# Converting two row blocks of a weight at a time, with a reordered start and extra products of ones

## The chip, the cores and the metric

The kernel runs on one core of a Trainium2 chip. The metric is the device time of one execution in microseconds (us). TensorE (PE) does matrix products and transposes, VectorE (DVE), ScalarE (ACT) and GpSimd (POOL) work on tiles of 128 partitions in SBUF, and SyncE (SP) issues the DMAs here. Each engine runs its own instructions in a fixed order and waits on semaphores for the others.

## The reference

Three layers follow each other on 4 batches of 576 positions with 512 channels:

```
scores = where(causal, -1e9, q k^T / 8 + min(-(cum_i - cum_j), 0))     # 32 heads of 64
attn   = softmax(scores) v                                             # cum = cumsum(relu(s))
xk, xr = mu * x + (1 - mu) * shift(x)                                  # token mix, x = attn
x2     = sigmoid(xr w_r) * (relu(xk w_k)^2 w_v)
u, v   = split(gelu(x2 w_in));  v_n = layernorm(v) * g_ln
out    = x2 + (u * (w_sg v_n + b_sg)) w_out
```

q, k, v and s are float32. The weights w_k, w_r, w_v, w_in and w_out arrive as float64, seen by the kernel as pairs of 32-bit words.

## The kernel before

Attention runs over 16 pairs of heads. The scores of a pair go through two PSUM tiles, VectorE adds the mask, scales and takes the minimum in one instruction (`fold`, L363; a second short instruction reads its accumulator), ScalarE takes the exponential (L389), PE transposes the rows and multiplies them by v. The first batch is done in two rounds of four pairs: pairs 0 to 3 with query blocks 0 to 2, then the same pairs with blocks 3 and 4. I number the folds from the start of the program; fold 20 ends the first round, fold 44 the second, and folds 45 to 50 open the second batch.

The next layer (`moe1`, L663 for its products) works in eight units of 288 columns. A product is made exact by splitting both sides into a high and a low float32r part and adding three products. Its operations are drawn in between those of attention, by a generator; a rate sets how many attention steps are taken per product, and a dependency without a semaphore puts the products of `moe1` behind the attention product issued last. The order in each queue is then settled by a scheduler with priorities.

Each weight has to be converted from float64 words to high and low parts (`convert`). For a 128-row block of 512 columns this takes seven instructions: ScalarE takes the absolute value of the high words (L111), VectorE bounds it (L115), shifts and masks (L116), puts in sign and exponent (L117) and the low word's bits (L118), ScalarE copies the high part, VectorE subtracts it (both through helpers, L71 and L74). The temporary `cvt` lives in the place of the tile `rt`, which `moe1` needs later. The 20 blocks of w_k, w_r and w_v are converted while the first batch's attention runs, w_in (8) and w_out (4) later. A VectorE copy of one element (L101) ties the load of a later block to a point in VectorE's order.

At the start, GpSimd clears the mask and the identity and selects their triangles, VectorE makes the running sum of s, and 18 products of ones (L246) occupy PE.

## Time and profile before

| quantity | value |
|---|---|
| runs | 703.83, 707.19 and 918.62 us, median 707.19 us |
| profiled execution | 701.49 us, of which the span of its instructions is 699.7 us |
| PE busy in the span | 663.8 us (95%) |
| DVE busy | 510.3 us (73%) |
| ACT busy | 406.5 us (58%) |
| POOL busy | 234.2 us (33%) |
| mean granted TensorE clock | 0.975 of full speed |

The shares are averages over stages. For a stage, read its own stretch: which engine is busy all the time there, and what the others wait for. A wait of an engine that has nothing urgent to do costs nothing.

### The profile page before, as it was taken

To read this page: it belongs to the slowest core of one execution; us is meant where nothing else is said; L and a number is where in the kernel's file an instruction comes from. 1 tells how busy PE (TensorE), PEld (TensorE's weight loads), DVE (VectorE), ACT (ScalarE), POOL (GpSimd) and SP (SyncE) were. 2 spreads that over 40 slices of the span, in tenths; PEclk is the share of its full clock that TensorE was granted. 3 is DMA by queue.
4 is the path that set the end of the run, shared out by engine and by line. 5 is a ranking of instruction groups with operands and counts; after the bars stand their busy time and mean duration, and the time that the engine had idled before them with its cause. 6 is when DMAs were issued, how large, how long until landed. Compare 5 with 4: busy or idle time off the path is not lost.

```text
span 699.7 us, 12939 instructions
## 1 busy us (share of the span) xinstructions
PE 663.8 (95%) x4598; PEld 624.9 (89%) x4598; DVE 510.3 (73%) x1227; ACT 406.5 (58%) x979; POOL 234.2 (33%) x232
## 2 busy tenths in 40 slices
PE   6888969999999989999899999999999999999998
PEld 3666969998998989999899989999998998998997
DVE  8989996887888887688776798744856564664543
ACT  5779767878878876888595544624523233233120
POOL 7024465645755765585542262120000000000000
PEclk8899968999999999999999999999999999999999
DMA  8996333344443333433201700004230300300101
GB/s 239 291 208 211 111 116 88 87 149 118 127 125 105 99 88 108 121 97 96 80 23 48 281 32 35 1 18 164 76 102 18 119 1 16 121 1 9 60 2 68
DMA packets 39833, 67.48 MB, mean 96 GB/s; under 512 B 6909, under 2 KB 23401, under 8 KB 39737
## 3 DMA queue, kind: packets, MB, share of 16 engines
q1 hardware_dynamic: 39768, 66.66, 32.1%
q8 instruction: 36, 0.59, 0.4%
q14 instruction: 29, 0.23, 0.1%
HBM read 51.85 MB, written 10.19 MB: 89 GB/s over the span
## 4 chain that ended last, share of the span: by engine, by line
PE 69%; ACT 7%; DVE 6%; DMA 2%; issue 1%; SPq 1%; POOL 0%; DVEq 0%; ACTq 0%; POOLq 0%
PE m L663 26%; PE po L676 7%; PE pu L676 7%; PE av L513 3%; PE t L528 3%; PE pg L914 2%; PE pg L915 2%; PE pg L913 2%; PE pv L851 2%; PE pv L852 2%; PE pv L850 2%; ACT pr L389 2%; PE s L348 2%; PE s L349 2%; DVE xf L602 1%
## 5 line engine op out<-in xcount | busy, mean ns | idle before, releaser
L74 POOL TENSOR_TENSOR xl<-xf,xh 128x288 fp32r<-128x288 f32 x64 | 70.1, 1106 | 88.8 <-ACT xh L71 47.7
L389 ACT ACTIVATE pr<-pr,nm 128x448 f32<-128x448 f32 (+4 forms) x144 | 84.9, 590 | 14.7 <-DVE nm L363 13.1
L663 PE MATMUL m<-xh,wk 128*128 128x288 f32 x512 | 81.6, 298 | 0.0
L663 PE MATMUL m<-kh,wv 128*128 128x288 f32 x512 | 80.1, 297 | 0.0
L363 DVE CUSTOM_DVE_ANT_0 pr<-s,mask 128x448 f32<-128x448 f32 (+4 forms) x144 | 63.6, 453 | 17.3 <-PE s L349 8.9
L663 PEld LDWEIGHTS m<-xh,wk 128*128 128x128 f32 x512 | 71.9, 189 | 0.9
L663 PEld LDWEIGHTS m<-kh,wv 128*128 128x128 f32 x512 | 71.8, 189 | 0.6
L348 PE MATMUL s<-qk 128*128 128x288 f32 (+4 forms) x144 | 46.8, 327 | 7.8 <-DVE nm L363 6.0
L602 DVE SCALAR_TENSOR_TENSOR xf<-xt,mu_sb,xf 128x288 f32<-128x288 f32 x64 | 47.3, 744 | 6.5 <-ACT xf L596 6.1
L532 DVE TENSOR_TENSOR ptl<-t,pth 128x512 fp32r<-128x512 f32 (+1 forms) x72 | 44.2, 616 | 7.0 <-ACT pth L531 6.8
L71 ACT CAST xh<-xf 128x288 fp32r<-128x288 f32 (+1 forms) x80 | 36.1, 480 | 22.4 <-DVE xf L602 13.7
L663 PE MATMUL m<-xl,wk 128*128 128x288 f32 x256 | 47.7, 299 | 0.0
L74 POOL TENSOR_TENSOR qk<-qld,qk 64x576 fp32r<-64x576 f32 (+1 forms) x28 | 39.2, 1401 | 21.2 <-DVE qk L71 9.4
L531 ACT CAST pth<-t 128x512 fp32r<-128x512 f32 (+1 forms) x72 | 37.9, 531 | 13.4 <-PE t L528 12.6
L349 PE MATMUL s<-qk 128*128 128x288 f32 (+4 forms) x144 | 44.6, 313 | 0.0
L596 ACT ACTIVATE xf<-xt,mu 128x288 f32<-128x288 f32 x64 | 33.9, 535 | 17.0 <-POOL xl L74 16.3
L663 PE MATMUL m<-kl,wv 128*128 128x288 f32 x256 | 43.4, 299 | 0.0
L624 ACT ACTIVATE kf<-m 128x288 f32<-128x288 f32 x64 | 26.0, 410 | 29.9 <-PE m L663 28.6
L663 PE MATMUL m<-xh,wr 128*128 128x288 f32 x256 | 40.5, 300 | 1.2 <-ACT rt L637 0.9
L676 PE MATMUL pu<-xh,wi 128*128 128x288 f32 x256 | 40.5, 296 | 0.2 <-ACT ut L876 0.2
L71 ACT CAST gh<-gf 128x288 fp32r<-128x288 f32 x32 | 13.9, 433 | 46.2 <-DVE gf L920 46.2
L528 PE MATMUL t<-ident,pr 128*128 128x128 f32 x252 | 39.1, 276 | 0.4 <-DVE ptl L532 0.2
(299 smaller groups left out, 1840.2 us busy)
## 6 DMA issues: line engine op xcount, KB each, us to landing
kld<-qkv SPq DMA_DIRECT2D x28, 288.0 KB
qld<-qkv SPq DMA_DIRECT2D x24, 288.0 KB
x_d<-rt SPq DMA_DIRECT2D x8, 576.0 KB
xf<-x_d SPq DMA_DIRECT2D x8, 576.0 KB
outT<-ot SPq DMA_DIRECT2D x32, 144.0 KB
vld<-qkv SPq DMA_DIRECT2D x24, 160.0 KB
qk<-qk SPq DMA_DIRECT2D x24, 144.0 KB
rb<-rd SPq DMA_DIRECT2D x24, 128.0 KB
```

The lines of the kernel that those rows point to most:

```text
L71: nc.scalar.copy(dst, src) if eng == "A" else nc.vector.tensor_copy(dst, src)
L74: (nc.gpsimd if pick(engines) == "P" else nc.vector).tensor_tensor(dst, a, b.bitcast(F32), ALU.subtract)
L348: nc.tensor.matmul(dst, qk[0][:, 0, qs], qk[0][:, 1, ks], start=True, stop=False)
L349: issued[0] = nc.tensor.matmul(dst, qk[1][:, 0, qs], qk[1][:, 1, ks], start=False, stop=True)
L363: nc.vector.tensor_tensor_reduce(out=dst, in0=src, in1=msk, scale=-0.125, scalar=first, op0=ALU.add, op1=ALU.min, accum_out=acc)
L389: i = nc.scalar.activation(dst, dst, AF.Exp, bias=nm[:, col : col + 1], scale=-1.0, accum_out=w.sm[:, col : col + 1])
L528: issued[0] = nc.tensor.transpose(bank[:, o : o + P], x, ident)
L531: nc.scalar.copy(pth[:, cols], bank[:, 0:o])
L532: nc.vector.tensor_tensor(ptl[:, cols], bank[:, 0:o], pth[:, cols].bitcast(F32), ALU.subtract)
L602: nc.vector.scalar_tensor_tensor(xf, xc, mu_sb[:, j, c : c + 1], xf, ALU.mult, ALU.add)
L663: i = nc.tensor.matmul(dst, w(x, c, m), xx[:, c], start=(n + c == 0), stop=(n == 2 and c == w.nk - 1))
L676: nc.tensor.matmul(dst, w(x, c, m), xx[:, c], start=(n + c == 0), stop=(n == 2 and c == w.nk - 1))
```

## The change

1. A weight's part now covers two row blocks. It is loaded by two DMAs into one tile and converted by seven instructions of 1024 elements instead of fourteen of 512. So w_k, w_r and w_v have 10 parts, w_in 4 and w_out 2. The look-ahead of loads goes from 5 blocks to 3 parts, and the rates at which conversions are drawn are halved (`C0`, `n % 2`, `n1`).
2. The temporaries move from the place of `rt` to tiles `xo0` and `xo1`, where the attention output of batches 1 and 3 will lie. Those tiles now hold two columns of 128 channels each; the even batches keep four tiles `xt0` to `xt3`, single-buffered.
3. The mask and the identity are cleared by VectorE instead of GpSimd, and the late clears of `qk` on GpSimd are put behind the two selections.
4. In the first four pairs, two products of ones follow each step's scores, 40 in all.
5. The first six absolute values are put behind an exponential each. The places for w_sg's parts change to suit the larger tiles.

```diff
-C0, RATE, LEAD, AHEAD = 0.7, 1.1, 0.0, 5
+C0, LEAD, AHEAD = 0.35, 0.0, 3
+GC = 6
+WJ, WN = 4, 2
-SLOTS = [("wk11", "wk21"), ("wk31", "wr00"), ("wr10", "wr20"), ("xh",), ("xl",)]
+SLOTS = ["wk01", "wk11", "wr00", "xh"]
...
-        raw = pool.tile([P, 512], I64, tag=name, name=name + "w")
+        raw = pool.tile([P, 2, 512], I64, tag=name, name=name + "w")
...
-            nc.vector.tensor_copy(raw.bitcast(F32)[:p, 0:1], after[:, 0:1])
-        nc.sync.dma_start(raw, src)
+            nc.vector.tensor_copy(raw.bitcast(F32)[:p, :, 0:1], after[:, 0:1].unsqueeze(1).to_broadcast([p, 2, 1]))
+        for i in range(2):
+            nc.sync.dma_start(raw[:, i], src[i * P : (i + 1) * P])
...
-        words = raw.bitcast(I32).rearrange("p (n t) -> p n t", t=2)
+        words = raw.bitcast(I32).rearrange("p c (n t) -> p (c n) t", t=2)
...
-        if GC and len(exps) > LC and done[0] < 2:
-            kind = mybir.DependencyInfo(mybir.DependencyClass.NoSync, mybir.DependencyReason.DATA)
-            tc.add_manual_dep(i.ins, exps[-1 - LC].ins.name, kind)
+        if 0 < len(exps) <= GC:
+            behind(i, exps[-1])
...
-        half = pool.tile([P, 2, 512], F32R, tag=name, name=name)
-        copy("A" if att is not None else "D", half[:, 0], t)
-        minus(ENG["cl"], half[:, 1], t, half[:, 0])
+        half = pool.tile([P, 2, 2, 512], F32R, tag=name, name=name)
+        hi, lo = (half[:, x].rearrange("p c n -> p (c n)") for x in range(2))
+        copy("A" if att is not None else "D", hi, t)
+        minus(ENG["cl"], lo, t, hi)
...
+        for i in i if eng is nc.gpsimd else ():
+            behind(i, made)
...
-    nc.gpsimd.memset(mask, 0.0)
+    nc.vector.memset(mask, 0.0)
...
-    make_identity(nc, ident)
+    nc.vector.memset(ident, 0.0)
+    made = nc.gpsimd.affine_select(
+        out=ident, in_=ident, compare_op=ALU.not_equal, fill=1.0, base=0, pattern=[[-1, P]], channel_multiplier=1
+    )
...
             exps.append(i)
+            if w.n < WJ:
+                for _ in range(WN):
+                    behind(nc.tensor.matmul(idle[:, 0:384], ones[:, 0:P], ones, start=True, stop=True), issued[0])
...
-                while w.p >= 8 and (w.p // 4 - 2, n % 4) not in mixed:
+                while b > 1 and not {(b - 2, x) for x in ((c, c + 1 - c % 2) if b % 2 else (c,))} <= mixed:
                     yield "wait"
-                w.xt = xtp.tile([P, S + 1], F32, tag=f"xt{n % 4}", name=f"xt{n % 4}", bufs=2)
-                xts.setdefault(w.p // 4, []).append(w.xt)
+                x = xts.setdefault(b, [])
+                if b % 2 == 0:
+                    x.append(xtp.tile([P, S + 1], F32, tag=f"xt{c}", name=f"xt{c}", bufs=1))
+                elif c % 2 == 0:
+                    two = xtp.tile([P, 2, S + 1], F32, tag=f"xo{c // 2}", name=f"xo{c // 2}", bufs=1)
+                    x += [two[:, 0], two[:, 1]]
...
-    temps = mw.tile([P, 2, 512], F32, tag="rt", name="cvt")
+    temps = [xtp.tile([P, 1024], F32, tag=f"xo{i}", name="cvt", bufs=1) for i in range(2)]
...
-            if n < 7:
+            if n < 7 and n % 2 == 0:
                 step(cvs, PC)
...
-    temps = w1p.tile([P, 2, 512], F32, tag="wk01", name="cvt")
-    cos = conversions([(wo, i, 0) for i in range(4)], lambda i: temps[:, i % 2])
+    temps = w1p.tile([P, 2, 1024], F32, tag="wr10", name="cvt")
+    cos = conversions([(wo, i, 0) for i in range(2)], lambda i: temps[:, i])
```

GpSimd at the start, before. `gt` is a table of bias rows, `qk_86` and `qk_87` are operand tiles, L255 is the mask's selection and masks.py:199 that of the identity:

```order
L254 MEMSET mask 128x768
masks.py:197 MEMSET ident 128x128
L159 MEMSET qk_87 64x640
...
L358 MEMSET sm 128x16
L718 MEMSET xt_262 128x1
L718 MEMSET xt_375 128x1
L255 ISA
L255 AFFINE_SELECT mask<-mask 128x128
masks.py:199 AFFINE_SELECT ident<-ident 128x128
```

GpSimd at the start, now (L264 and L275 are the selections):

```order
L166 MEMSET qk_87 64x640
L370 MEMSET sm 128x16
...
L478 MEMSET rcp 128x128
L307 MEMSET gt 48x576
L308 MEMSET gt 48x576
L307 MEMSET gt 48x576
L308 MEMSET gt 48x576
L167 MEMSET qk_87 1x640
L264 ISA
L264 AFFINE_SELECT mask<-mask 128x128
L275 AFFINE_SELECT ident<-ident 128x128
```

Two clears left GpSimd and eight went behind the selections, but four clears of `gt` and some small ones came ahead of them.

VectorE from fold 40 on, before. `pr_91`, `pr_90` and `pr_89` are the rows of scores that a fold writes, `cvt` the temporary, `wv_...` a converted block of w_v, `qk_1084` an operand of the next attention stage, `avt` and `sm` belong to attention:

```order
L118 SCALAR_TENSOR_TENSOR cvt<-wv50w,cvt 128x512
L398 RECIPROCAL rc<-sm 128x8
L115 TENSOR_SCALAR cvt<-cvt 128x512
L363 ISA pr_90,nm<-s,mask 128x448
...
L116 TENSOR_SCALAR cvt<-cvt 128x512
L74 TENSOR_TENSOR wv_823<-cvt,wv_823 128x512
L117 SCALAR_TENSOR_TENSOR cvt<-wv60w,cvt 128x512
L118 SCALAR_TENSOR_TENSOR cvt<-wv60w,cvt 128x512
L115 TENSOR_SCALAR cvt<-cvt 128x512
L455 TENSOR_TENSOR avt<-av,rc 128x256
L363 ISA pr_91,nm<-s,mask,nh 128x288
```

VectorE from fold 38 on, now:

```order
L118 SCALAR_TENSOR_TENSOR cvt<-wv30w,cvt 128x1024
L74 TENSOR_TENSOR qk_1027<-kld,qk_1026 64x576
...
L375 ISA pr_91,nm<-s,mask,nh 128x288
L375 ISA nm 128x1
L71 CAST qk_1026<-qld 128x576
L74 TENSOR_TENSOR wv_829<-cvt,wv_829 128x1024
L617 SCALAR_TENSOR_TENSOR xf<-xt_359,mu_sb,xf 128x288
L375 ISA pr_91,nh<-s,mask 128x288
```

The last conversion instruction now stands at fold 40, the last one before stood at fold 48; 11 of the 100 stood behind fold 40, now 1 of 50 (the L74 shown).

PE in the first pair, now. L358 is a product of scores, L439 a transpose, L407 the added products of ones:

```order
L358 MATMUL s<-qk_86 128x192
L407 LDWEIGHTS ones
L407 MATMUL warm<-ones 128x384
L407 LDWEIGHTS ones
L407 MATMUL warm<-ones 128x384
L439 MATMUL t<-ident,pr_89 128x128 x2
L439 MATMUL t<-ident,pr_88 128x128
```

Apart from these 40 pairs of rows the products of `moe1` and those of the scores stand in the same places to each other as before.

## Rows read from the trace of the kernel before

**Rows 1.** Windows by stage: busy time and instructions of each engine, granted clock, DMA.

```profile
20.00:60.00 40.00, 31.99 (x167) 23.30 (x167) 37.81 (x124) 32.59 (x90) 7.78 (x12) 0.92 0.99 267
69.00:90.00 21.00, 18.87 (x145) 18.36 (x145) 20.93 (x43) 16.27 (x38) 10.13 (x9) 1.00 0.43 129
113.00:700.00 587.00, 573.72 (x4096) 551.60 (x4096) 405.04 (x953) 322.45 (x770) 184.34 (x158) 1.00 0.26 79
```

**Rows 2.** Windows from the second round's end on, columns as in Rows 1.

```profile
89.70:98.86 9.16, 3.92 (x19) 2.88 (x19) 9.16 (x18) 6.30 (x13) 8.09 (x7) 0.75 0.34 96
98.86:111.33 12.47, 12.47 (x57) 12.27 (x57) 10.27 (x23) 7.64 (x17) 5.75 (x5) 0.50 0.30 83
111.33:117.50 6.17, 5.46 (x46) 5.15 (x45) 4.22 (x13) 4.75 (x13) 1.43 (x2) 1.00 0.29 86
```

**Rows 3.** Timeline of VectorE, first round: start, busy us, line, operation.

```profile
31.48 0.14 DVE L101 COPY wr20w<-cvt 128x1 f32<-128x1 f32 x1
31.55 0.68 DVE L118 SCALAR_TENSOR_TENSOR cvt<-wk11w,cvt 128x512 int32<-128x512 int32 x1
32.15 0.68 DVE L74 TENSOR_TENSOR wk<-cvt,wk 128x512 fp32r<-128x512 f32 x1
32.75 0.14 DVE L101 COPY wr30w<-cvt 128x1 f32<-128x1 f32 x1
...
33.95 0.42 DVE L115 TENSOR_SCALAR cvt<-cvt 128x512 f32<-128x512 f32 x1
34.29 0.48 DVE L363 CUSTOM_DVE_ANT_0 pr<-s,mask 128x320 f32<-128x320 f32 x1
```

**Rows 4.** Groups by shape, VectorE, 0 to 115 us: busy, mean ns, idle before.

```profile
L115 DVE TENSOR_SCALAR cvt<-cvt 128x512 f32<-128x512 f32 x20 | 12.3, 613 | 0.7 <-ACT cvt L111 0.7
L363 DVE CUSTOM_DVE_ANT_0 pr<-s,mask 128x448 f32<-128x448 f32 x9 | 5.4, 605 | 0.0
L363 DVE CUSTOM_DVE_ANT_0 pr<-s,mask 128x128 f32<-128x128 f32 x4 | 1.1, 279 | 0.0
```

**Rows 5.** Timeline of VectorE, two instructions of which the second needs the first.

```profile
55.65 0.84 DVE L117 SCALAR_TENSOR_TENSOR cvt<-wr20w,cvt 128x512 int32<-128x512 int32 x1
56.52 1.11 DVE L118 SCALAR_TENSOR_TENSOR cvt<-wr20w,cvt 128x512 int32<-128x512 int32 x1
```

**Rows 6.** Timeline of all engines, start of the kernel.

```profile
1.46 0.59 DVE L158 MEMSET qk<- 64x640 f32 x1 [0.19 <-issue]
1.93 0.20 POOL masks.py:197 MEMSET ident<- 128x128 f32 x1
2.13 0.59 DVE L159 MEMSET qk<- 64x640 f32 x1
5.39 0.74 POOL L255 TENSOR_SCALAR_AFFINE_SELECT mask<-mask 128x128 f32<-128x128 f32 x1
8.54 0.49 DVE L363 CUSTOM_DVE_ANT_0 pr<-s,mask 128x320 f32<-128x320 f32 x1
11.09 0.66 ACT L111 ACTIVATE cvt<-wk10w 128x512 f32<-128x512 f32 x1 [1.81 <-DMA wk10w<-w_k]
12.21 0.56 ACT L389 ACTIVATE pr<-pr,nm 128x320 f32<-128x320 f32 x1
```

**Rows 7.** Timeline of PE's weight loads beside the products of ones, start of the kernel.

```profile
5.14 0.15 PEld L246 LDWEIGHTS <-ones 128*128 128x128 bf16 x1 [0.17 <-issue]
5.46 0.63 PEld L246 LDWEIGHTS <-ones 128*128 128x128 bf16 x4 [0.17 <-issue]
```

**Rows 8.** Timeline of PE, groups of eight products at either speed.

```profile
87.89 1.22 PE L663 MATMUL m<-xh,wr 128*128 128x288 f32 x8
...
99.90 1.81 PE L432 MATMUL av<-vb,pth 128*128 128x64 f32 x8
113.75 1.00 PE L432 MATMUL av<-vb,pth 128*128 128x64 f32 x8
...
117.50 1.28 PE L663 MATMUL m<-xh,wr 128*128 128x288 f32 x8
```

**Rows 9.** Windows of 4 us, first round, columns as in Rows 1.

```profile
8.00:12.00 4.00, 1.63 (x6) 0.85 (x6) 3.21 (x15) 1.84 (x5) 3.71 (x11) 1.00 0.97 216
12.00:16.00 4.00, 2.02 (x8) 1.26 (x8) 3.96 (x14) 3.66 (x13) 1.93 (x4) 0.55 0.92 282
56.00:60.00 4.00, 2.73 (x15) 1.61 (x15) 3.97 (x12) 4.00 (x10) 1.20 (x2) 1.00 0.80 263
```

More of the change, by code (lines that the diff above doesn't have):

```diff
@@ L231, in block_kernel @@
     fetch(-1)
-    for c in range(max(1, E1)):
-        load_words(wk, c % 4, c // 4)
+    load_words(wk, 0, 0)
     gate_d = dram.tile([48, 2, 4, S], F32, name="gate_d")
@@ L288, in block_kernel @@
             rest(x, a, b, nc.gpsimd, nc.gpsimd)
-    for c in range(max(1, E1), AHEAD):
-        load_words(wk, c % 4, c // 4, after=cur)
+    for c in range(1, AHEAD):
+        load_words(wk, c % 2, c // 2, after=cur)
     tc.cur_priority += SECOND + GT
@@ L751, in block_kernel @@
     att = attend()
[L752 to L758 removed]
+    temps = [xtp.tile([P, 1024], F32, tag=f"xo{i}", name="cvt", bufs=1) for i in range(2)]
     cvs = conversions(
[L761 to L762 removed]
+        [(wk, c, n) for n in range(2) for c in range(2)] + [(wr, c, 0) for c in range(2)] + [(wv, c, 0) for c in range(4)],
+        lambda i: temps[i % 2],
         loaded=AHEAD,
@@ L833, in block_kernel @@
             temps = w2.tile([P, 5, 512], F32, tag="vt", name="cvt")
-            lws = conversions([(wi, c, n) for n in (1, 0) for c in range(4)], lambda i: temps[:, i % 5])
-            lws = chain(lws, x_load(0))
-        if w2 is not None and n % PACE == 0:
-            next(lws, None)
+            lws = conversions([(wi, c, n) for n in (1, 0) for c in range(2)], lambda i: temps[:, i % 2 * 2 : i % 2 * 2 + 2].rearrange("p c n -> p (c n)"))
+            lws, n1 = chain(lws, x_load(0)), 0
+        if w2 is not None:
+            n1 += 1
+            if n1 % PACE == 1 and n1 // PACE % 2 == 0 or n1 > 8 * PACE and n1 % PACE == 1:
+                next(lws, None)
     for _ in lws:
@@ L889, in norm @@
         nc.vector.tensor_tensor(rs, rs, t1, ALU.mult)
-        vh, vl = ([xtp.tile([P, DM], F32R, tag=f"xt{t}", name=n) for t in range(4)] for n in ("vh", "vl"))
+        vh = [xtp.tile([P, DM], F32R, tag=f"xt{t}", name="vh", bufs=1) for t in range(4)]
+        vl = [xtp.tile([P, 2, DM], F32R, tag=f"xo{t}", name="vl", bufs=1) for t in range(2)]
+        vl = [vl[t // 2][:, t % 2] for t in range(4)]
         v4 = const.tile([P, DM], F32R, tag="mask", name="v4")
@@ L937, in block_kernel @@
         nc.gpsimd.memset(mv[:, 4], 1.0)
+    places = [w1p.tile([P, 3, S], F32R, tag=t, name="wg") for t in SLOTS[:3]]
+    places = [x[:, i] for x in places for i in range(3)] + [xtp.tile([P, S], F32R, tag=SLOTS[3], name="wg")]
     wg = [[], []]
-    for c, tags in enumerate(SLOTS):
-        if len(tags) == 2:
-            halves = [w1p.tile([P, S], F32R, tag=t, name=f"wg{c}") for t in tags]
-        else:
-            place = xtp.tile([P, 2, S], F32R, tag=tags[0], name=f"wg{c}")
-            halves = [place[:, 0], place[:, 1]]
+    for c in range(5):
+        halves = places[2 * c : 2 * c + 2]
         for hf in range(2):
```

37 lines of the change are left out of this document (17 added, 20 removed).

## The prediction

> **What bounds the kernel now.** I read the windows by stage first, since the busy shares of the whole span mix stages with different limits. From 113 us on PE is busy 573.7 of 587.0 us at the granted clock 1.00 [rows 1]: that part is PE's, and time saved before it moves its end by as much, since its products stay the same. Before that VectorE is the full engine: 37.8 of 40 us from 20 to 60, and 20.9 of 21 from 69 to 90, with PE idle for 8.0 and 2.1 us [rows 1]. What fills it is the conversion of w_k, w_r and w_v beside the folds of attention. Then comes a stretch of another kind [rows 2]. From 89.7 to 98.9 us VectorE is full and PE has work for 3.9 of 9.2 us; by its end the clock has fallen. From 98.9 to 111.3 PE is busy all the time at the granted clock 0.50, which is 1.2 GHz, and VectorE has 2.2 us free. Eight products of 64 columns take 1.81 us there and 1.00 us at 113.75 [rows 8]. So the first 113 us are VectorE's, but for some 12 us that belong to PE at half speed.
>
> **The change, part by part.**
>
> *Merged conversions.* A VectorE step from one instruction's start to the next is 0.60 us for 512 elements (31.55, 32.15, 32.75) and 0.34 us for the bounding L115, which takes two elements at a time (33.95 to 34.29) [rows 3]. Folds of 448 and 128 elements take 605 and 279 ns [rows 4], so an element costs 326/320 = 1.02 ns, 512 cost 0.52 us, and 0.60 - 0.52 = 0.08 us of a step is fixed; for L115 it is 0.34 - 0.26 = 0.08 again. Of the three weights, 20 blocks with five VectorE instructions each become 10 parts: 100 instructions become 50, on a full engine. That removes 50 x 0.08 = 4.0 us. The copies that tie the loads go from 15 to 8, at steps of 0.07 us (31.48 to 31.55) [rows 3]: 0.5 us. ScalarE's 40 instructions become 20, but it is busy 32.6 of 40 us [rows 1], less than VectorE, so I count nothing.
>
> The VectorE page of the Trainium skill (VectorE: DVE Perf Modes, section The TRN2 errata) gives a fixed term of about 150 cycles per instruction, 156 ns at its 0.96 GHz. By that alone the merge would save 50 x 0.156 = 7.8 us. The folds' durations agree with the page (279 - 128 x 1.02 = 148 ns), the steps don't, because the next instruction starts 0.08 us before the end of the last [rows 3]; the sum goes by the steps.
>
> *Clears on VectorE.* Clearing 640 columns takes a step of 0.67 us (1.46 to 2.13) [rows 6], so 768 take 0.80; the identity's 128 took 0.20 on GpSimd [rows 6]. Together 1.0 us more on VectorE ahead of the running sum. At best nothing of it shows, if s lands later than I think; I take all of it, since VectorE runs through from there to the first fold at 8.54 us.
>
> *Mask selected first.* It isn't, in GpSimd's queue: two clears of about 0.9 us left, but four of `gt` came ahead of the selections. The mask's selection started at 5.39 us [rows 6] and I expect it within 0.7 us of that. Nothing gained or lost: VectorE reads the mask only after the running sum.
>
> *First exponential.* Before, ScalarE waits 1.81 us for the second load of w_k and starts its first exponential at 12.21 us, 3.2 us after its fold ended (8.54 + 0.49) [rows 6]. Now the exponentials go first, and I expect the first one at about 10. This shortens the first pair but not VectorE's sum: the conversion that ran between the folds now runs behind them. I take 0; if PE and ScalarE were the path there, it would be worth at most 2.
>
> *Products of ones.* 40 of 384 columns. At full speed one takes 0.16 us (0.63 for four), at half speed 0.32 (5.14 to 5.46) [rows 7]: 6.4 to 12.8 us of PE in the first 50 us. PE has 8.0 us free between 20 and 60, and more before: it is busy 1.63 and 2.02 of 4 us from 8 to 16 [rows 1, 9]. They hide there, because a transpose behind them waits for an exponential anyway. If that cover were gone, each pair would hold the next transposes by 0.3 us, 20 x 0.3 = 6 us. They may keep the clock, which is 0.55 from 12 to 16 us [rows 9]; VectorE is full then, so this pays nothing by itself.
>
> *Conversions earlier.* The last conversion instruction moves from fold 48 to fold 40. Before, 11 of the 100 stood behind fold 40, 4 of them at 0.34 and 7 at 0.60: 5.6 us. Now it is one of 1024 elements, 1.1 us. So VectorE is 5.6 - 1.1 = 4.5 us lighter behind fold 40, and as much heavier before it.
>
> *Places and pacing.* The second batch's output tiles are now free only when the temporaries are. The second batch's clear of `xo0` waits for the last part that uses it, w_v's third, whose last instruction stands at fold 30, so it is long past; batch 3's first tile waits for two mixes instead of one, some 24 products of 0.16 us (1.28 for eight [rows 8]), 4 us, while PE has other products. w_in and w_out are converted behind 113 us, where VectorE is busy 405 of 587 us [rows 1]. I count 0 for these, at worst 4. SP's queue loads the same bytes by the same number of transfers; two loads of q and k go ahead of the bias rows now, 1 us at worst for pair 1, which waits for its predecessor longer than that.
>
> **The sum** on VectorE is -4.0 - 0.5 + 1.0 = -3.5 us, made against the profiled execution of 701.49 us: 698.0. That execution lies 5.7 us below the median of the three runs and 2.3 below the lowest. The median is drawn up by one run of 918.62, so I set the timed runs 2.3 us above the profile: **700.3 us**.
>
> **The rivals.**
>
> *The clock stays up.* Lighter by 4.9 us between folds 32 and 40 (23 instructions of 512, 8 x 0.34 + 15 x 0.60 = 11.7 us, against 7 of 1024, 2 x 0.60 + 5 x 1.12 = 6.8), VectorE may feed PE densely enough. Then the 12.5 us at half speed become 6.2, VectorE needs 10.3 - 4.5 = 5.8, and as fold 40 comes 4.5 - 3.5 = 1.0 us later, the end moves by -6.3 + 1.0 = -5.3: 698.5 us timed. For it: from 56 to 60 us PE is busy 2.73 of 4 and keeps 1.00 [rows 9]. Against: PE fell at 1.63 of 4, and 3.9 of 9.2 that become 3.9 of some 7 lie between.
>
> *Slower: the early work is not paid back.* If the clock falls as before, the 12.5 us are PE's own and don't shrink with VectorE's load. Then the 1.0 us by which fold 40 is late stays. If beside this the products of ones hold the transposes at half of their 20 places, 3 us come on top: 701.5 + 1.0 + 3.0 = 705.5 us profiled, 4 above before's profile, and 707.8 timed. It decides at PE's free time from 20 to 60: with the ones at 0.32 us they take 30 x 0.32 = 9.6 of the 8.0 us there, at 0.16 only 4.8.
>
> *More per instruction.* Where an instruction needs the one ahead of it, it starts only at its end: 55.65 + 0.84 = 56.49, the next at 56.52 [rows 5]. And L115 averages 613 ns against 420 undisturbed [rows 3, 4]. If merging saves the full 0.15 us, 50 x 0.07 = 3.5 us more: 694.5 profiled, 696.8 timed. Against: most conversion instructions stand between others. The page's 156 ns above would lead here too.
>
> **How the numbers follow.** 2% of the median is 14.1 us, about what a measurement of this kernel can tell from no change. I give the sum 0.42, the clock 0.22, more per instruction 0.10, the slower case 0.20, and 0.06 to things not seen. The range takes in the clock and the merge together (698.5 - 3.5 = 695.0, less the first exponential's 2 and the runs' 2 = 691) and the slower case (707.8) with 1 us: 691 to 709. Faster by over 2% (below 693.0) needs two of the gains at once: 0.08. Slower by over 2% needs a wait that I don't see: 0.04.
>
> **What would show it.** VectorE's steps at 1024 elements of 1.12 to 1.14 us; the first exponential near 10 us; the second group of products with w_r, which follows the first (87.89) at 117.50 [rows 8], at 112 to 115. Right next to this, the clock from 90 to 111: at 1.00 throughout it is the clock's case. The prediction is wrong if the second w_r group still starts at 117.5 or later, or if PE loses more than 13.3 us behind it.

## The result and the profile after

The changed kernel takes 709.3 us (median of 9 runs, 707.69 to 713.86) beside 702.32 us for the kernel before on the same chip: a ratio of 1.0105, 95% interval [1.0078, 1.0132], some 7 us slower. The prediction was 700.3 us with a range of 691 to 709. The profiled execution took 707.69 us, its span is 705.9 us; before it was 701.49 and 699.7.

First the windows by stage of the changed kernel (columns as in Rows 1; 20 to 60, 69 to 90 and 113 to 700 answer to [rows 1]):

```profile
8.00:40.00 32.00, 23.95 (x111) 17.11 (x112) 24.93 (x67) 23.00 (x57) 7.53 (x11) 0.79 0.91 280
20.00:60.00 40.00, 31.05 (x167) 23.24 (x168) 34.68 (x86) 28.19 (x68) 8.89 (x9) 0.87 0.82 258
69.00:90.00 21.00, 20.78 (x162) 19.74 (x161) 19.87 (x33) 16.34 (x36) 14.45 (x13) 1.00 0.30 94
0.00:113.00 113.00, 92.12 (x536) 72.82 (x537) 100.29 (x220) 82.27 (x191) 54.56 (x72) 0.91 0.62 187
113.00:700.00 587.00, 575.17 (x4090) 553.69 (x4089) 399.98 (x910) 322.16 (x763) 178.84 (x158) 0.99 0.25 78
```

Two windows of the kernel before that Rows 1 does not hold:

```profile
8.00:40.00 32.00, 22.88 (x112) 16.64 (x113) 30.34 (x101) 24.26 (x67) 10.11 (x20) 0.83 0.94 264
0.00:113.00 113.00, 90.06 (x502) 73.31 (x502) 105.27 (x275) 84.05 (x211) 49.88 (x74) 0.86 0.67 188
```

Up to 113 us VectorE's work fell from 105.27 to 100.29 us: 5.0 us are saved, more than the 3.5 of the sum. But from 8 to 40 us VectorE is busy 24.93 of 32 us where it was busy 30.34. It stands still for 7.1 us instead of 1.7. The saved time came back as idle time of the engine that was taken for the full one.

PE's w_r groups, which the prediction named as its test (timeline of PE, changed kernel; [rows 8] has 87.89 and 117.50):

```profile
95.99 1.30 PE L678 MATMUL m<-xh,wr 128*128 128x288 f32 x8
...
118.44 1.27 PE L678 MATMUL m<-xh,wr 128*128 128x288 f32 x8
```

The first group is 8.1 us late, the second only 0.9. Between them the kernel before ran at half speed (clock 0.50 from 98.86 to 111.33, [rows 2]); the change has the clock at 1.00 from 80 to 100 us and at 0.91 from 100 to 120.

The first fold and the first exponential (timeline of VectorE and ScalarE; [rows 6] has 8.54 and 12.21):

```profile
9.88 0.49 DVE L375 CUSTOM_DVE_ANT_0 pr<-s,mask 128x320 f32<-128x320 f32 x1
...
10.53 0.56 ACT L401 ACTIVATE pr<-pr,nm 128x320 f32<-128x320 f32 x1
```

To see where the rest is lost I line the traces up by work: PE streams the same columns of products in both kernels, products of ones left out, so I compare when the same share of them has been streamed. Each entry is how late a kernel's profiled execution is against the kernel before, at the moments at which that one stood at 34, 52, ... us (1, 2, 5, 7, 30, 49, 52, 70 and 100% of the columns):

| kernel | 34 | 52 | 83 | 116 | 274 | 398 | 416 | 522 | 696 | timed ratio [95%] |
|---|---|---|---|---|---|---|---|---|---|---|
| change | 6.3 | 6.4 | 8.2 | 0.9 | 1.0 | 2.1 | 5.7 | 6.6 | 5.8 | 1.0105 [1.0078, 1.0132] |
| e1 | 5.3 | 6.5 | 8.3 | 2.3 | 2.9 | 2.9 | 1.8 | 3.1 | 2.2 | 1.0044 [1.0021, 1.0066] |
| e2 | 5.7 | 5.8 | 7.6 | 0.4 | -0.1 | -0.1 | 3.2 | 5.7 | 4.9 | 1.0134 [1.0104, 1.0163] |
| e3 | 9.0 | 15.9 | 18.3 | 14.5 | 21.3 | 21.3 | 24.9 | 25.7 | 24.8 | 1.0354 [1.0320, 1.0388] |
| e5 | 2.8 | 4.7 | 9.5 | 7.7 | 8.7 | 8.7 | 12.1 | 14.4 | 13.6 | 1.0200 [1.0174, 1.0227] |
| e6 | 5.3 | 5.4 | 7.1 | -0.1 | -0.3 | 0.7 | 2.4 | 4.1 | 3.3 | 1.0087 [1.0055, 1.0119] |
| e7 | -1.3 | -4.6 | 0.8 | -1.2 | 9.8 | 10.1 | 9.1 | 9.7 | 9.7 | 1.0136 [1.0102, 1.0170] |
| e8 | 0.6 | 5.4 | 7.1 | 3.1 | 5.3 | 5.3 | 8.7 | 11.1 | 10.3 | 1.0146 [1.0112, 1.0179] |
| e9 | 7.3 | 8.5 | 13.2 | 1.6 | 1.6 | 1.6 | 0.5 | 1.6 | 0.7 | 0.9989 [0.9968, 1.0010] |
| e10 | 1.4 | 2.1 | 8.6 | 0.9 | 6.7 | 6.7 | 7.4 | 9.8 | 8.9 | 1.0177 [1.0138, 1.0216] |
| e11 | -3.2 | -0.8 | 3.5 | 0.3 | 0.0 | 1.1 | 1.8 | 2.4 | 1.6 | 1.0029 [1.0010, 1.0048] |
| e12 | 5.0 | 12.2 | 20.2 | 6.2 | 6.2 | 7.3 | 6.2 | 8.0 | 7.1 | 1.0100 [1.0080, 1.0120] |
| e13 | -1.0 | 0.5 | 0.4 | 0.3 | -0.1 | 0.3 | -0.8 | -0.3 | -0.3 | 1.0007 [0.9988, 1.0025] |
| e14 | -1.2 | -0.4 | 4.4 | 1.3 | 1.0 | 2.1 | 1.0 | 1.8 | 0.9 | 0.9998 [0.9978, 1.0017] |
| e15 | -3.6 | -0.2 | 3.3 | 3.2 | 8.5 | 8.5 | 7.4 | 9.4 | 8.5 | 1.0112 [1.0080, 1.0144] |
| e16 | -0.5 | 1.7 | 5.4 | -1.6 | -2.5 | -1.0 | -2.1 | -2.4 | -3.3 | 0.9950 [0.9924, 0.9976] |
| e17 | -3.0 | -0.5 | 3.4 | 0.3 | -0.1 | 1.0 | 0.0 | 0.6 | -0.3 | 0.9996 [0.9976, 1.0017] |
| e18 | 3.2 | 6.8 | 8.7 | 4.5 | 5.0 | 5.0 | 3.9 | 5.4 | 4.5 | 0.9982 [0.9951, 1.0013] |
| e19 | 0.2 | 3.4 | 5.9 | 1.4 | 1.5 | 1.5 | 0.4 | 1.7 | 0.8 | 1.0013 [0.9986, 1.0041] |

One execution is one sample: the change and e1 have the same queues up to 375 us, the change and e2 up to 491, and they stand at 0.9, 2.3 and 0.4 us at 116. A difference of 2 us there is no finding by itself; the timed ratios decide (0.0014 is 1 us). The ± of a difference of two ratios below joins their two intervals by squares (the root of the sum of their squared half widths). In the table the change loses 0.9 us by 116, 1.1 between 274 and 398, 3.6 between 398 and 416 and 0.9 between 416 and 522, and gains 0.8 behind.

### The profile page after: what moved, and what is told of

It reads as the page before. It is cut to its first block, busy times and chain, and to the rows that moved or that the text cites. A ratio compares the mean times of both kernels' runs of the same rounds, so it can differ in the third digit from the quotient of the medians.

```text
span 705.9 us, 12858 instructions
## 1 busy us (share of the span) xinstructions
PE 669.5 (95%) x4638; PEld 628.5 (89%) x4638; DVE 501.2 (71%) x1132; ACT 404.4 (57%) x953; POOL 233.4 (33%) x230
## 3 DMA queue, kind: packets, MB, share of 16 engines
HBM read 51.85 MB, written 10.19 MB: 88 GB/s over the span
## 4 chain that ended last, share of the span: by engine, by line
PE 71%; DVE 12%; ACT 7%; DMA 3%; POOL 2%; issue 2%; SPq 1%; DVEq 0%; POOLq 0%; ACTq 0%
PE m L678 27%; PE pu L691 7%; PE po L691 7%; PE av L528 3%; PE t L543 3%; PE pg L933 2%; PE pg L935 2%; PE pg L934 2%; PE s L360 2%; PE pv L868 2%; PE pv L870 2%; PE pv L869 2%; PE s L361 2%; DVE pr L375 2%; DVE xf L617 2%
## 5 line engine op out<-in xcount | busy, mean ns | idle before, releaser
L74 POOL TENSOR_TENSOR xl<-xf,xh 128x288 fp32r<-128x288 f32 x64 | 69.1, 1090 | 95.9 <-PE m L678 46.5
L375 DVE CUSTOM_DVE_ANT_0 pr<-s,mask 128x288 f32<-128x288 f32 (+4 forms) x144 | 63.7, 453 | 22.3 <-PE s L361 9.8
L71 ACT CAST xh<-xf 128x288 fp32r<-128x288 f32 (+1 forms) x80 | 36.0, 478 | 25.7 <-DVE xf L617 11.6
L74 POOL TENSOR_TENSOR qk<-qld,qk 64x576 fp32r<-64x576 f32 (+1 forms) x28 | 40.8, 1458 | 21.3 <-DVE qk L71 5.5
L678 PEld LDWEIGHTS m<-xh,wr 128*128 128x128 f32 x256 | 37.4, 197 | 3.3 <-ACT rt L652 3.2
L678 PEld LDWEIGHTS m<-xl,wk 128*128 128x128 f32 x256 | 38.6, 190 | 0.7 <-issue 0.4
```

The costliest lines, as they stand in the source:

```text
L71: nc.scalar.copy(dst, src) if eng == "A" else nc.vector.tensor_copy(dst, src)
L74: (nc.gpsimd if pick(engines) == "P" else nc.vector).tensor_tensor(dst, a, b.bitcast(F32), ALU.subtract)
L375: nc.vector.tensor_tensor_reduce(out=dst, in0=src, in1=msk, scale=-0.125, scalar=first, op0=ALU.add, op1=ALU.min, accum_out=acc)
L678: i = nc.tensor.matmul(dst, w(x, c, m), xx[:, c], start=(n + c == 0), stop=(n == 2 and c == w.nk - 1))
```

## The experiments

**The stop at 404 us.** Timeline of PE, ScalarE and GpSimd in the changed kernel, in brackets what ended the idle time before an instruction:

```profile
401.30 5.02 POOL L74 TENSOR_TENSOR xl<-xf,xh 128x288 fp32r<-128x288 f32 x2 [12.69 <-PE m L678]
...
405.60 0.54 ACT L611 ACTIVATE xf<-xo,mu 128x288 f32<-128x288 f32 x1 [3.17 <-POOL xl L74]
406.35 0.54 ACT L611 ACTIVATE xf<-xo,mu 128x288 f32<-128x288 f32 x1 [0.22 <-POOL xl L74]
406.79 0.69 ACT L652 ACTIVATE rt<-m 128x288 f32<-128x288 f32 x2
...
407.24 1.32 PE L678 MATMUL m<-xh,wr 128*128 128x288 f32 x8 [2.94 <-ACT rt L652]
```

And in the kernel before:

```profile
399.19 4.16 POOL L74 TENSOR_TENSOR xl<-xf,xh 128x288 fp32r<-128x288 f32 x2 [12.21 <-PE m L663]
...
402.18 0.54 ACT L596 ACTIVATE xf<-xt,mu 128x288 f32<-128x288 f32 x1 [1.42 <-POOL xl L74]
...
403.06 1.32 PE L663 MATMUL m<-xh,wr 128*128 128x288 f32 x8 [0.93 <-ACT rt L637]
```

Read it from the bottom. PE waits for a product bank that the tanh on ScalarE (L652) empties. ScalarE is stuck one instruction earlier, at a mixing product for the next unit (L611), whose place is free only when GpSimd has subtracted the low part xl. The first subtraction takes 4.3 us until ScalarE goes on (401.30 to 405.60), where the 64 of the program average 1.09 us, while VectorE converts w_in beside it, now in steps of 1024 elements. The same wait existed before; it was 0.93 us long. Behind the wait PE runs at half speed for a while: the granted clock of the change is 0.58 from 408 to 412 us.

**e1_xl_vector** takes the subtraction from GpSimd.

```diff
-            minus(ENG["xl"], xl[:, c], xf, xh[:, c])
+            minus(ENG["xl"] if att is not None else "D", xl[:, c], xf, xh[:, c])
```

> The changed kernel, but once attention has ended the low parts xl of the mixed inputs (L619) are subtracted on VectorE, not on GpSimd. Theory: at 401 us GpSimd's two subtractions take 5.0 us for some 2 because VectorE's 1024-element conversions run beside them; ScalarE's mixing products wait for them, the tanh that frees the products' bank stands behind those on ScalarE, so PE stands still for 2.94 us and then runs 3.4 us at half speed. Then PE's wait before the third w_r group of that unit is under 0.6 us, the clock stays at 1.00 from 395 to 420 and the time falls by 3 to 4 us (ratio to before near 1.005). Rival: VectorE itself is the full engine there, so the subtractions wait on VectorE as long as they did on GpSimd: PE still stands for 2 us or more and the time stays within 1 us of the change.

Windows from 395 to 420 us, the kernel before, the change and then e1:

```profile
395.00:420.00 25.00, 24.07 (x159) 22.45 (x159) 23.48 (x46) 14.15 (x31) 14.51 (x6) 1.00 0.37 133
```

```profile
395.00:420.00 25.00, 22.06 (x150) 21.47 (x149) 23.48 (x33) 14.78 (x30) 11.71 (x5) 0.93 0.28 98
```

```profile
395.00:420.00 25.00, 25.00 (x174) 23.99 (x173) 24.48 (x40) 15.42 (x30) 0.00 (x0) 1.00 0.31 111
```

PE no longer stops and the clock stays at 1.00. Instead of losing 3.6 us there, e1 gains 1.1; timed it is 0.0061 ± 0.0035 (4.3 ± 2.4 us) faster than the change. The theory is shown. The 1.1 us are a wait that the kernel before has too (e13 below), so the change's own cost here is the 3.6 us.

**e6_halves_late** keeps GpSimd and shortens the steps: each of a conversion's operations is issued twice, for 512 elements; e5 below does the same during attention.

```diff
+        cut = (slice(0, 512), slice(512, 1024)) if att is None else (slice(0, 1024),)
+        for z in cut:
+            nc.vector.tensor_scalar(t[:, z], t[:, z], 2.0**-15, None, ALU.max)
...
```

> The changed kernel, but after attention (w_in and w_out) each conversion step is issued as two instructions of 512 elements; places, loads and pacing stay. Theory: at 400 us it is the length of VectorE's instructions that starves GpSimd's subtractions, and at 505 us short subtractions for wg and rt stand behind steps of 1.2 us. Then from 395 to 420 us the loss against the kernel before is under 1.5 us (the change lost 3.8), from 498 to 520 under 0.5 (the change 1.1), and the time falls by 3 us or more against the change. Rival: it is the density of VectorE's work, not the length: the same loss at 400 us within 1 us, because the conversions still stand there at the same time.

It lost 1.7 us from 398 to 416, between the two expectations. But PE's wait hardly fell, from 2.94 to 2.53 us; the rest of the gain is that PE did not fall to half speed behind it (granted clock from 408 to 412 us 1.00, in the change 0.58). VectorE, ScalarE and PE in the change, then in e6:

```profile
404.47 0.45 DVE L71 CAST kh<-kf 128x576 fp32r<-128x576 f32 x1
406.17 0.52 DVE L617 SCALAR_TENSOR_TENSOR xf<-xo,mu_sb,xf 128x288 f32<-128x288 f32 x1 [1.25 <-ACT xf L611]
```

```profile
402.45 0.68 DVE L124 SCALAR_TENSOR_TENSOR cvt<-wi11w,cvt 128x512 int32<-128x512 int32 x1
403.82 0.54 ACT L618 ACTIVATE xf<-xo,mu 128x288 f32<-128x288 f32 x1 [2.77 <-POOL xl L74]
405.45 1.32 PE L685 MATMUL m<-xh,wr 128*128 128x288 f32 x8 [2.53 <-ACT rt L659]
```

In both, ScalarE goes on 0.7 us after VectorE's unbroken row of instructions ends (404.92 and 405.60, 403.13 and 403.82); in the kernel before GpSimd came through at 402.18 while VectorE went on. So for the wait it is the row that counts, as the rival has it, more than the length of one step. Timed, the gain is 0.0018 ± 0.0042: unclear. From 416 to 522 it lost as much as the change or more, so length is not the cause there.

**e13_before_xl** is e1's line in the kernel before.

> The kernel before with e1's edit alone: xl subtracted on VectorE once attention has ended. Theory: its PE waits 0.93 us at 403 us for the same reason as the change waits 2.94; with the edit that wait goes and the time falls by about 1 us (ratio 0.997 to 0.999), nothing else moves. Rival: the conversions of w_in that VectorE does there come later by the subtractions' 3 us and the wait moves to the first products with w_in: same time or up to 1 us later.

It gained 1.1 us between 398 and 416 in the trace, and gave half of it back by 522. The timed ratio, 1.0007 [0.9988, 1.0025], shows no gain: the expected 1 us (0.9986) lies just outside the interval, a smaller gain is not excluded.

**e2_wo_place** and **e17_rawg** (the latter on e14's base) turn to the 0.9 us behind 498. In the change PE waits for an addition to rt that stands behind a conversion of w_out (timelines of PE and VectorE):

```profile
503.79 1.22 DVE L117 SCALAR_TENSOR_TENSOR cvt<-wk00w,cvt 128x1024 int32<-128x1024 int32 x1
504.93 0.45 DVE L664 TENSOR_TENSOR rt<-m,rt 128x288 f32<-128x288 f32 x1
...
505.43 2.38 PE L678 MATMUL m<-kh,wv 128*128 128x288 f32 x16 [0.93 <-DVE rt L664]
```

```diff
-SLOTS = ["wk01", "wk11", "wr00", "xh"]
+SLOTS = ["wk11", "wr00", "wr10", "xh"]
...
-    temps = w1p.tile([P, 2, 1024], F32, tag="wr10", name="cvt")
+    temps = w1p.tile([P, 2, 1024], F32, tag="wk01", name="cvt")
```

> The changed kernel, but the temporaries for w_out stand in the place of wk01 (free after the last product with w_k) and the parts wg in wk11, wr00 and wr10. Theory: in the change the temporaries wait for the last product with w_r (498 us), 6 us later than the last with w_k (491.6), so the conversion of w_out falls among the last four additions to rt, and PE waits 0.93 us for one of them. Then that wait is gone (under 0.2 us) and the time falls by about 1 us. Rival: the late loads of rawg hold ScalarE and VectorE there whatever the place: the wait stays or moves to the first gate products, and the time is the same within 0.5 us.

The conversions came 11 us earlier (490.25 for the first, 501.48 in the change), this wait went, but PE then waited 0.68 us for a tanh and 1.49 us for ScalarE's table load behind the last copy of rawg. From 416 to 522 it lost 2.5 us; timed it is 0.0029 ± 0.0040 slower than the change, where 1 us less was expected. The theory fell: the place decides which wait it is, not whether there is one.

```diff
+    raw4 = xtp.tile([P, 4, HD], F32, tag="xl", name="rawg", bufs=2)
...
-            raw = mw.tile([P, HD], F32, tag="xf", name="rawg", bufs=2)
+            raw = raw4[:, 2 * c + hf] if c < 2 else mw.tile([P, HD], F32, tag="xf", name="rawg", bufs=2)
```

> e14 with room for the first four loads of w_sgT (rawg) in a place of xl that is free, so that they need not wait for one another; the other six go through the two places as before. Theory: at 505 us PE waits because ten loads through two places take 13.6 us (492.5 to 506.1 in the change) and ScalarE's copies of them stand ahead of the tanh, and the table load behind the last of them; with four out of the chain it is 5 us shorter and the loss between 498 and 520 us falls from 0.9 us to 0.2 or less. Rival: the conversions of w_out among rt's additions cost it, not the loads: the loss stays within 0.3 us.

e17 lost 0.6 us from 416 to 522 beside e14's 0.8, at equal timed ratios (0.9996, 0.9998). The rival holds, as far as one can tell 0.2 us. What the 0.9 us are remains open.

**What merging is worth: e5_halves_early.** The edit is e6's with `att is not None`.

> The changed kernel, but while attention runs each conversion step is issued as two instructions of 512 elements (ScalarE's and VectorE's alike); places, loads and pacing of the double parts are kept. The sum of the prediction: 50 VectorE instructions more, 50 x 0.08 = 4 us more up to 113 us. Theory now: the step of 0.60 us is cheaper for what waits behind it than one of 1.2 us. In the change the reciprocals and folds of the first pairs stand behind steps of 1.2 to 1.5 us (rc at 30.83), and from 20 to 40 us VectorE idles 4.8 us because PE waits for them; with halves fold 20 (52.1 us) comes 2 to 4 us earlier, and at the second w_r group the time is within 2 us of the change's. If the prediction's sum holds, fold 40 and the second w_r group come 2 to 4 us later than in the change.

At 34 us e5 was 3.5 us ahead of the change, in the theory's direction, but at 116 it was 6.8 behind, and timed 0.0095 ± 0.0038 (6.7 ± 2.7 us) slower. Windows from the start to the end of fold 50, the kernel before, the change and e5:

```profile
0.00:119.16 119.16, 96.08 (x553) 79.34 (x554) 109.48 (x289) 88.94 (x223) 52.42 (x77) 0.87 0.64 181
```

```profile
0.00:120.11 120.11, 99.05 (x593) 79.51 (x594) 103.78 (x232) 87.01 (x203) 56.73 (x75) 0.91 0.59 179
```

```profile
0.00:126.92 126.92, 104.20 (x593) 83.25 (x594) 108.40 (x282) 89.73 (x223) 45.64 (x75) 0.89 0.56 170
```

With 50 instructions more VectorE is busy 4.6 us longer, 0.09 us each: on VectorE merging saves what the sum gave it (4.0 us), not the 7.5 of the rival "more per instruction". What that is worth at the end is less sure: with halves the clock fell to 0.60 between 100 and 113 us, in the change it was 0.87, and VectorE's order is another from 19 us on. If it is worth 4 us, everything else in the change costs some 11, where the prediction had half a microsecond.

**The first pairs: products of ones, and a wait.**

```diff
-WJ, WN = 4, 2
+WJ, WN = 0, 0
```

> The changed kernel without the 40 products of ones beside the first four pairs. Theory: they lie in PE's idle time and cost nothing by themselves, and the clock from 94 to 111 us does not hang on them, which end by 50 us; PE's second w_r group starts within 1.5 us of the change's, and the time is the same within 1.5 us. Rival 1: they hold the transposes and scores at half speed, from 30 to 40 us above all: without them fold 20 (52.1 us in the change, 45.5 before) comes 3 us or more earlier. Rival 2: they keep the clock up early: without them the half-speed stretch before 40 us is longer than the change's 3.4 + 10.2 us, and the stretch from 94 to 111 falls to half again (end later by 3 us or more).

e3 lost 17.5 us (0.0249) against the change, which looked like the second rival. The timeline of VectorE and of SyncE's queue in e3 says otherwise:

```profile
41.91 0.17 DVE L101 COPY wv00w<-cvt 128x2 f32<-128x2 f32 x1 [7.42 <-issue]
```

```profile
34.82 0.79 SPq L316 DMA_DIRECT2D gate_d<-gt  x2
42.11 0.35 SPq L103 DMA_DIRECT2D wv00w<-w_v  x1
```

w_v's first part lies where `gt` was, so the copy that ties its load waits until gt has been stored, with folds behind it. Without the ones the scheduler had put that store at 34.82 us instead of 26.72 and 29.92. The bracket in e3 names no releaser; in the change, where the same copy waits 1.29 us, it names the store:

```profile
35.38 0.17 DVE L101 COPY wv00w<-cvt 128x2 f32<-128x2 f32 x1 [1.29 <-DMA gate_d<-gt]
```

In the kernel before the copy comes at 39.10 and waits for nothing. **e10_ahead2** and **e11_ahead2_no_ones** move the copy back, with and without the ones:

```diff
-C0, LEAD, AHEAD = 0.35, 0.0, 3
+C0, LEAD, AHEAD = 0.35, 0.0, 2
```

> The changed kernel with AHEAD = 2: double parts are loaded two ahead instead of three (four blocks, where the kernel before had five). The copy on VectorE that ties the load of w_v's first part to its place, which is gt's, then stands some 30 instructions later in VectorE's queue. In the change it waits there 1.29 us for the store of gt (35.38), in the kernel without ones 7.42 us, in e8 4.92 us, with folds and conversions behind it. Theory: this wait is a part of the 5 us that VectorE saved and lost again in idle time from 20 to 40 us: without it that idle time falls from 4.8 to 3.5 us or less, and the lag at 35 us against the kernel before from 6.3 to 5 or less; by 116 us it shows as at most 1.5 us, because the clock from 94 on decides there. Rival: with two ahead ScalarE waits for weights that have not landed, and the lag at 116 us is 2 us or more above the change's 0.9.

> The changed kernel with AHEAD = 2 and without the 40 products of ones. Without ones alone the kernel ended 19 us later than the change, but 7.4 us of that were the wait for the store of gt, which stood later in SP's queue, and some 7 us two statistics steps of VectorE beside GpSimd (3.46 and 3.87 us for 9 elements, at 183 and 272 us). Theory: the ones are worth 3 to 6 us through the clock before 116 us, and the rest came with the other order: against e10 this kernel is 3 to 6 us late at 116 us, and no single wait of VectorE there is over 2 us. Rival 1: the ones are worth it all through the clock: 12 us or more late against e10 at 116 us. Rival 2: nothing: within 1.5 us of e10 at 116 us.

In e10 the copy came at 47.14 without a wait; at 34 and 52 us the lag fell from 6.3 and 6.4 to 1.4 and 2.1, and at 116 it was the same 0.9. In e11 it was 0.3: by 116 us the ones show no worth beyond the scatter of 2 us (second rival), and e3's loss came with its order. Yet e10 was timed 0.0148 ± 0.0043 slower than e11, and 0.0072 ± 0.0047 slower than the change. It lost 5.8 us between 116 and 274, in stretches that the ones don't touch (last section). **e9_more_ones_xl** (e1 with `WJ, WN = 8, 2`), **e12_four_ones** (`8, 4`) and **e7_before_ones_xl** (the kernel before with e1's line and the change's ones) go on with this.

> The changed kernel with e1's edit (xl on VectorE after attention) and the products of ones beside the first eight pairs instead of four. Theory: ones keep the clock up wherever PE waits; the half-speed stretches at 64 and 108 us (3.4 us each in the change, 6.8 at 107.6 in e1) vanish, and the end comes 1 to 3 us earlier than e1's (ratio 0.999 to 1.003). Rival: behind 45 us PE's free time is too short and the ones delay what others wait for: the same as e1 or up to 4 us later.

> The changed kernel with e1's edit and four products of ones after each score step of the first eight pairs (e9 had two). Theory: what is left of the loss before 116 us is PE at half speed from 17 to 41 us (17 us of it in e9): twice the ones keep it busy enough that the half-speed stretches before 60 us fall below 7 us in all, and the lag at 116 us falls from e9's 1.6 to -1 or less, the time to a ratio of 0.994 to 0.997. Rival: PE is then full with ones: at half speed eight of them take 2.6 us per pair's two steps, the scores behind them come late, and the end is 2 to 6 us later than e9's.

> The kernel before with two edits at places far apart: two products of ones after each score step of the first four pairs, as in the change, and xl subtracted on VectorE once attention has ended, as in e1. Taking the ones out of the change cost 19 us by the end, so they hold the clock. Theory: on the kernel before they shorten its 10.2 us at half speed from 12.4 us on (and may shorten the 17.1 us from 94 on); the lead against before at 116 us is 2 to 6 us. The second edit takes away its wait of 0.93 us at 403: the lead grows by 0.5 to 1 us there, time 695 to 699 (ratio 0.990 to 0.996). Rival: the ones are worth something only with the long steps, which starve PE; with before's steps of 512 they only take PE's time: no lead at 116 us, or up to 3 us late.

e9 was 3.9 ± 2.2 us faster than e1, its clock 1.00 from 60 to 113 us; e12 had the clock at 1.00 from 40 on and was 7.8 us slower than e9, VectorE idle for 20 of the first 113 us (13 in e9): the rival. e7 led by 4.6 us at 52 and 1.2 at 116, then lost 11.0 by 274: neither the expected lead of 2 us nor the time came. More ones raise the clock, but the time goes up or down with the order that comes with them.

**The start: e8_clears.** Mask and identity are cleared on GpSimd again (`nc.gpsimd.memset`).

> The changed kernel, but the mask and the identity are cleared on GpSimd again, ahead of the selections. The change's first fold comes 1.4 us later than before (9.88, 8.54), of which the prediction put 1.0 down to the two clears on VectorE. If that holds, the first fold comes at 8.8 to 9.2 us; whether the end gains it too is open: the theory of the second half of the losses says no (PE's end hangs on the clock from 94 on), so the time is within 1.5 us of the change. Rival: the running sum waits for s or for GpSimd, not for the clears: first fold at 9.7 or later.

The running sum began 1.4 us earlier, but the first fold at 10.19, not 9.88, because a copy on VectorE was slowed beside GpSimd's later clears. Timed, e8 is 0.0041 ± 0.0043 slower than the change: unclear. Timeline of VectorE in e8, then in the change:

```profile
7.07 2.01 DVE L286 COPY qk<-cum 1x320 f32<-1x320 f32 x1
```

```profile
8.90 0.42 DVE L286 COPY qk<-cum 1x320 f32<-1x320 f32 x1
```

**e14_base, e15_start, e16_abs_first.** e14 is e11 with e1's line. e15 undoes the order of the clears too (the two clears on GpSimd and no `behind(i, made)`), e16 only this:

```diff
-GC = 6
+GC = 0
```

> The changed kernel without the products of ones, with AHEAD = 2 (as e11) and with xl on VectorE once attention has ended (as e1). If repairs at places far apart add up: e11's lag of 0.3 us at 116 us, and at 405 us a gain of 1 us instead of e11's loss of 0.6: 1.6 us earlier than e11, ratio 1.000 to 1.002. Rival: the order of the rest shifts with it and the gain is lost behind 420 us: within 0.5 us of e11 (1.003).

> e14 with the start as it was before: mask and identity cleared on GpSimd, and GpSimd's late clears no longer held behind the identity's selection. Theory: the clears' order costs the first fold 1.3 us (9.9 against 8.5), and VectorE's and PE's chain carries it on: first fold at 8.4 to 8.8 us and the lag at 116 us 1 us or more below e14's. Rival: by 116 us it is gone, since what limits there is the clock from 94 on: lag within 0.7 us of e14's.

> e14 with GC = 0: the first conversions' absolute values no longer stand behind the first exponentials. Theory: holding them back makes VectorE idle in the first pairs (1.07 + 0.41 us from 12 to 14 in the change, and the conversions land between later folds); without it VectorE is busier from 8 to 20 us by 1 us or more and the lag at 52 us falls by 1 us or more, at 116 us by up to 1. Rival: the exponentials first are worth what the prediction allowed (0 to 2 us): the lag at 23 us rises by 1 to 2 us and at 116 us by 0 to 2.

e14 is as fast as the kernel before: the two repairs add up. e15 has its first fold at 8.54 us, and was 8.0 us slower than e14 for all that: theory fallen, the early start did not survive; e15 has the long step of the last section. e16 was 0.0048 ± 0.0032 (3.4 ± 2.3 us) faster than e14 and is faster than the kernel before. Windows of e14 and of e16:

```profile
8.00:40.00 32.00, 23.17 (x103) 17.23 (x104) 24.51 (x74) 22.88 (x63) 7.29 (x12) 0.78 0.80 231
```

```profile
8.00:40.00 32.00, 23.70 (x105) 18.45 (x105) 29.32 (x83) 24.23 (x66) 7.60 (x13) 0.77 0.92 269
```

With the hold VectorE is busy 24.5 of these 32 us, as in the change; without it 29.3, near the 30.3 of the kernel before. The hold is on fewer instructions than I took it for. It lasts while no more than six exponentials have been issued, not for six absolute values, and the drawing of three attention steps per conversion leaves two of these inside: that of `wk00` behind the third exponential and that of `wk10` behind the sixth. The sixth belongs to the second pair, as each pair has five in this round, and that pair's scores wait for their bias rows (the transfer in brackets is inferred; `cur_d` holds the rows of the pair behind). Timeline of PE and ScalarE in the change:

```profile
21.32 0.78 PE L358 MATMUL s<-qk 128*128 128x320 f32 x2 [2.68 <-DMA qk<-cur_d]
...
22.73 0.56 ACT L401 ACTIVATE pr<-pr,nm 128x320 f32<-128x320 f32 x1 [0.71 <-DVE nm L375]
...
23.30 1.17 ACT L112 ACTIVATE cvt<-wk10w 128x1024 f32<-128x1024 f32 x1
```

In e16 the same conversion starts as soon as its weight is there, ahead of the sixth exponential (18.77), and VectorE begins on it at 18.59:

```profile
16.77 1.13 ACT L112 ACTIVATE cvt<-wk10w 128x1024 f32<-128x1024 f32 x1 [0.98 <-DMA wk10w<-w_k]
```

In e14 these are 20.87 and 26.11 us. But the gain did not come by the path that was expected: at 34 and 52 us e16 was 0.7 and 2.1 us later than e14, not earlier. It passed e14 between 83 and 116 us, where less conversion was left (VectorE busy 5.82 of 13 us from 100 to 113, in e14 10.41) and the granted clock was 0.87 instead of 0.57.

**e18_change_abs_first** (e1 with GC = 0) and **e19_ones_abs_first** (e16 with the ones):

> e1 (the change with xl on VectorE after attention) with GC = 0: the first absolute values are no longer held behind the first exponentials. Theory: holding them cost the change 3 us before 116 us whatever stands beside it: lag at 116 us from e1's 2.3 to -1 or less, ratio from 1.0044 to 1.000 or less. Rival: with the ones PE and ScalarE set the pace of the first pairs, and the lag at 116 us stays within 1.5 us of e1's.

> e16 (no ones, two parts ahead, xl on VectorE, GC = 0; ratio 0.995) with the change's 40 products of ones put back. Theory: the ones lie in PE's free time and the clock before 94 us does not set the end: lag at 116 us within 1.5 us of e16's -1.65, ratio 0.993 to 0.998. Rival 1: they hold scores and transposes: 2 us or more late against e16 at 116 us. Rival 2: they keep the clock up: 2 us or more early.

e18 is 0.0062 ± 0.0038 (4.4 ± 2.7 us) faster than e1, as the theory has it; VectorE was busy 28.0 of 32 us from 8 to 40, e1 25.5. The lag of its profiled execution doesn't show it: at 116 us it was 4.5, not -1 or less, and that execution took 706.45 us, among the slowest of twelve. The twelve lie in two groups of six, 696.75 to 699.49 and 703.17 to 708.11 us, so the size of the gain is less certain than its interval says. e19 is 4.4 ± 2.7 us slower than e16 and 3.0 us later at 116: the first rival, though not by 116 us alone.

## Why the prediction was wrong

Timed, the change lost 7.4 us (0.0105). Two of the prediction's terms, both set to 0, cost about 4 us each; undoing both (e18) gives 0.9982 [0.9951, 1.0013], and the sum's -3.5 us (0.9950) lies just outside this interval. In the profiled execution the lag is 0.9 us at 116, where the sum had -3.5, and 4.9 us more come behind it, where the prediction had none.

- *First exponential* is the earlier of the two steps that failed: "This shortens the first pair but not VectorE's sum: the conversion that ran between the folds now runs behind them. I take 0." The sum of VectorE's work was indeed unchanged. Its idle time was not: the second part's conversion (`wk10`) hangs on the second pair's first exponential, and that pair waits for a transfer, so VectorE stood still while work was there. It was idle 5.4 us more than before from 8 to 40 us. Without the hold 2.5 (e18 against e1) and 4.8 us (e16 against e14) of VectorE's work came back into these 32 us; the look-ahead of three parts had a share too (e10, busy 27.24, 2.3 us more than the change). The hold's cost, timed, was 4.4 and 3.4 us. By which path it reached the end is not shown: e16 gained only where the clock of 83 to 116 us was better, e18's trace shows no gain, and both change the order of PE's queue as well. The exponential itself came at 10.53, as foretold. I looked at what the hold brings forward and not at what the last of the held instructions waits for.
- *Places and pacing*, "w_in and w_out are converted behind 113 us, where VectorE is busy 405 of 587 us [rows 1]. I count 0 for these, at worst 4": 3.6 us in the trace at one place, and 4.3 ± 2.4 us timed by a repair that also takes away the old wait. The mean over 587 us hid that VectorE is busy 23.48 of 25 us from 395 to 420, in both kernels, and that PE already waited 0.93 us there through GpSimd and ScalarE. This step is the better shown of the two. The same term gave the second pair at worst 1 us for its bias rows, hidden behind the pair ahead: PE waited 2.68 us for them, though the pair's first fold (22.14) was not later than before (22.73).
- *Merged conversions*: right in kind and step. VectorE's steps of 1024 elements take 1.14 us and those of the shift and mask 0.60 (25.31 to 26.45 to 27.05, below). Undoing them cost VectorE 4.6 us, 4.0 foretold, and 6.7 ± 2.7 us timed, with a lower clock and another order beside it. The tying copies went from 17 to 8, not from 15, which is 0.1 us.

```profile
25.31 1.22 DVE L117 SCALAR_TENSOR_TENSOR cvt<-wk01w,cvt 128x1024 int32<-128x1024 int32 x1
26.45 0.69 DVE L116 TENSOR_SCALAR cvt<-cvt 128x1024 int32<-128x1024 int32 x1
27.05 0.51 DVE L617 SCALAR_TENSOR_TENSOR xf<-xt,mu_sb,xf 128x288 f32<-128x288 f32 x1
```

- *Clears on VectorE*: 1.0 us foretold, the first fold is 1.34 us late. e8 and e15 show no gain at the end from undoing it, but both brought other losses.
- *Products of ones*: nothing beyond the scatter by 116 us in e10 and e11, as foretold, 3.0 us later in e19 than in e16. Timed, they moved kernels by 4 to 17 us either way, with the order of the queues changing beside them, which the term left out.
- *Rivals.* The clock did stay up, and the lag fell by some 7 us between 83 and 116, but this was only what had been lost before. The slower rival has the right sign and nearly the size, by luck: it needed PE's half-speed stretch to stay, and that went. "More per instruction" is not borne out: it wanted 7.5 us of VectorE's time (50 x 0.15), and e5 shows 4.6.
- The step from the profile to the timed runs was 2.3 us by the three runs at hand; beside the change the kernel before came out at 702.32 us, 0.8 above its profile. This put the forecast 1.5 us too high and has no part in the sign.
- Both conditions for being wrong came true: the second w_r group at 118.44, and PE idle for 15.6 us behind 113 (577.35 of 592.9 busy) where it was 13.3.

What stays open: the path by which the hold cost its 3 to 4 us, the 1.1 us between 274 and 398, the 0.9 behind 498, and how much the ones cost or give apart from the order they bring. An order of the queues that changes with an edit is a rival to each of the early experiments, and none of them holds it fixed.

## What to carry to other kernels

A dependency that orders work behind events of another chain can cost what the latest of these events is late: find that event in the trace before setting the term to 0 because the engine's work is unchanged. A mean over a long stage does not price a collision; look up the window in which the moved work will stand, and who already waits there. And when one edit makes a kernel much slower, look for the single longest wait before believing the edit's own story: e3's loss began with a place shared with a table that was stored late.
